# Attention, feed-forward and soft mixture on one core: scores in four quarters of the array, TensorE's order from tile 20 on taken from the program

## The chip, the cores and the metric

The kernel runs on one core of one Trainium2 chip. The core has five engines that work side by side: TensorE (PE, matrix products; its weight loads are listed as PEld), VectorE (DVE), ScalarE (ACT), GpSimd (POOL) and SyncE (SP), which here only issues transfers. Each takes its instructions strictly in the order in which they were put into its queue, and waits at an instruction until what that one needs is there. The metric is the device time of one execution in microseconds (us).

## What is computed

The reference has three stages, each on 3072 tokens of width 512 (4 sequences of 768):

```python
# 1 attention: 32 heads of 64; a query sees 16 keys to either side and 24 block maxima
k_sum = k.reshape(B, H, nb, block, D).max(axis=3)
v_sum = v.reshape(B, H, nb, block, D).mean(axis=3)
scores = concat([where(|i-j| < 16, scale * q @ k.T, -1e9), scale * q @ k_sum.T + log(32)])
x = softmax(scores) @ concat([v, v_sum])
# 2 feed-forward, 512 -> 2048 -> 512
h = x @ w_in;  x = (h * cos(h)) @ w_out
# 3 soft mixture of 8 experts with 4 slots each
logits = x @ phi
d = softmax over tokens(logits);  slot_input = d.T @ x
slot_out[e] = relu(slot_input[e] @ w1[e]) @ w2[e]
out = softmax over slots(logits) @ slot_out
```

All is float32 at the reference's accuracy; the large products are made of three products in the rounded format fp32r (high by high, low by high, high by low).

## The kernel before

**Feed-forward, the trunk.** Six batches b of 512 tokens by 16 slices of the hidden width give 96 tiles s. `mm1(s)` is 12 products of 128x512 into one of two "h" banks of PSUM (L375 to 385); `act1(s)` (L388 to 400) reduces h on DVE (two instructions, L398 and L399) and takes the sine on ACT; `act2(s)` (L403 to 410) multiplies by h on DVE (L405, which frees the h bank), rounds to gh on ACT (L408) and takes the rest gl on POOL (L409); `mm2(s)` (L412 to 423) is 12 products into four acc banks and runs two tiles later. I write H(s) and A(s) for these two dozens of products. `split_w` makes the rounded and the rest part of a slice's weights on ACT (L370) and POOL (L371). In the first 16 tiles the weights are also converted, in three steps on ACT and DVE (L125, L126, L134, L135).

**Background.** Attention is cut into 24 groups g of 8 units (a unit is 64 queries of one sequence against 120 keys, for the two heads of a pair, which lie on rows 0 to 63 and 64 to 127). Groups 0 to 3 are done at the start, the others beside the tiles: scores `att_A(g, j)` in two halves j of four units (8 products 64x64 by 64x120 into one bank, head hh in the array's rows and columns 64*hh; a DVE instruction, L286, scales, adds the mask and writes S), then the row maximum, the exponentials on ACT, the norm, the transposes `att_C` ("tr", L333), the products with v `att_D` ("av", L351). The third stage runs one batch behind: x is transposed ("xt", L447), multiplied by phi ("lt", L455), and so on ("ltt", "dt", "sp"). All of these, and the sums of v ("vs"), share the two banks of one pool, `ps_m`, tag "m": whoever asks for a bank gets the one of the two that was taken longest ago, once its last reader is done.

**What sets the order.** The program emits the tiles in a loop; background work is placed in it by half-steps (two per tile), with a table of offsets (`OC`, `OD`, `MC` and others). The framework's scheduler then orders each engine's queue with a model of its own; in the kernel before it does so for all engines from start to end, so a product of the background can stand anywhere among a tile's products. On the chip this order is fixed.

Of the kernel before, what the change touches and what calls it, by code (L numbers as in the profile page):

```python
# [10 lines left out]
F32 = mybir.dt.float32  # L11
# [4 lines left out]
ALU = mybir.AluOpType  # L16
# [3 lines left out]
B, H, S, D = 4, 8, 768, 64  # L20
# [3 lines left out]
QB = 64  # L24
# [4 lines left out]
KC = KL + NSUM  # L29
# [8 lines left out]
CL = 4  # L38
CP = 0
EE = mybir.EngineType  # L40
MAN = None
PD = 1
PRE = "F I K0 Q0 M K1 Q2 W0 K2 Q1 K3 A B0 Q3 B1 B2 V0 V2 W1 V1 V3 W2 m k0 k1 s0 e0 s2 e2 k2 k3 v X0 X2 X1 X3 s1 t0 e1 s3 t2 e3 d0 t1 d2 t3 d1 d3 c0 G4 G5 W3 c1 W4 c2 w0 c3 W5 a4 a5 f V4 X4 V5 X5 S P"
NACT = 0
NABS = 0
S1 = 1
# [29 lines left out]
def body(ctx: ExitStack, tc: tile.TileContext, q0, qk, kT, vn, vx, w, phi, ex, cst, out):  # L76
    nc = tc.nc
# [5 lines left out]
    m2 = ctx.enter_context(tc.tile_pool(name="m2", bufs=1))  # L83
    ps_acc = ctx.enter_context(tc.tile_pool(name="ps_acc", bufs=1, space=PSUM))
    ps_h = ctx.enter_context(tc.tile_pool(name="ps_h", bufs=2, space=PSUM))
    ps_m = ctx.enter_context(tc.tile_pool(name="ps_m", bufs=2, space=PSUM))
# [3 lines left out]
    att = att_cm.__enter__()  # L90


    NM = 6 * KC
    mask = att.tile([128, 6, KC], F32, name="mask", tag="mask", bufs=1)
    ident = const.tile([128, 128], F32, name="ident")
    sel = const.tile([128, 32 + 256], F32, name="sel")
    avg = const.tile([128, 52], F32, name="avg")
    phis = const.tile([128, 4, 32], F32, name="phis")
# [8 lines left out]
    dsel = sel[:, 0:32]  # L107
# [36 lines left out]
    ksums, vsums, grp = {}, {}, {}  # L144
# [125 lines left out]
            nc.scalar.activation(d["S"][:, u, :], d["ps", j][:, c:c + KC], AF.Exp, bias=d["mx"][:, u:u + 1],  # L270
                                 scale=SCALE, accum_out=d["sm"][:, u:u + 1])

    def att_A(g, j):
        d = grp[g]
        if j == 0:
            if g % 2 == 0:
                grp["S", g // 2] = att.tile([128, 16, KC], F32, name=f"S{g}", tag="S")
            d["S"] = grp["S", g // 2][:, 8 * (g % 2):8 * (g % 2) + 8, :]
        ps = ps_m.tile([128, 512], F32, name=f"sc{g}_{j}", tag="m")
        heads = [slice(64 * hh, 64 * hh + 64) for hh in range(2)]  # L280
        for u in range(4):
            for r in heads:
                t = d["qk"][r, j, u, :]
                nc.tensor.matmul(ps[r, u * KC:(u + 1) * KC], t[:, 0:QB], t[:, QB:], start=True, stop=True)  # L284
        c = (g // 2) % 3
        nc.vector.scalar_tensor_tensor(  # L286
            out=d["S"][:, 4 * j:4 * j + 4, :].rearrange("p w c -> p (w c)"),
            in0=ps[:, 0:4 * KC], scalar=SCALE,
            in1=mask[:, c:c + 4, :].rearrange("p w c -> p (w c)"),
            op0=ALU.mult, op1=ALU.add)  # L290

    def att_max(g, negate=False):
        d = grp[g]
# [48 lines left out]
    def att_D(g):  # L342
        d = grp[g]
        ps = bank(f"av{g}") if g < 4 else ps_m.tile([128, 512], F32, name=f"av{g}", tag="m")
        for j in range(2):
            aT = d["aT", j]
            for u in range(4):
                c = 256 * j + QB * u
                for hh in range(2):
                    r = slice(64 * hh, 64 * hh + 64)  # L350
                    nc.tensor.matmul(ps[r, c:c + QB], d["v"][:, j, u, r],  # L351
                                     aT[:, 128 * u + 64 * hh:128 * u + 64 * hh + 64], start=True, stop=True)
        b, o = g // 4, 256 * ((g // 2) % 2)
        if b not in xh:
            xh[b] = xres.tile([128, 4, TB], F32R, name=f"xh{b}", tag="xh", bufs=2)
            xl[b] = xres.tile([128, 4, TB], F32R, name=f"xl{b}", tag="xl", bufs=2)
        p = 2 * (g % 2)
        ps = ps.rearrange("p (j c) -> p j c", j=2)
        hi, lo = (x[b][:, p:p + 2, o:o + 256] for x in (xh, xl))
        nc.scalar.copy(hi, ps)  # L360
        nc.vector.tensor_tensor(out=lo, in0=ps, in1=hi, op=ALU.subtract)  # L361
# [14 lines left out]
    def mm1(s):  # L376
        f = s % NF
        h = ps_h.tile([128, TB], F32, name=f"h{s}", tag="h")
        hi, lo = wi[f]
        for t in range(4):  # L380
            c = slice(128 * t, 128 * t + 128)
            nc.tensor.matmul(h, hi[:, c], xh[s // NF][:, t, :], start=t == 0, stop=False)  # L382
            nc.tensor.matmul(h, hi[:, c], xl[s // NF][:, t, :], start=False, stop=False)  # L383
            nc.tensor.matmul(h, lo[:, c], xh[s // NF][:, t, :], start=False, stop=t == 3)  # L384
        hps[s] = h

# [25 lines left out]
    def mm2(s):  # L412
        f = s % NF
        gh, gl = gs.pop(s)
        hi, lo = wo[f]
        if f == 0:
            for t in range(4):
                acc[t] = ps_acc.tile([128, 512], F32, name=f"acc{s}_{t}", tag=f"acc{t}")
        for t in range(4):
            c = slice(128 * t, 128 * t + 128)  # L420
            nc.tensor.matmul(acc[t], gh[:, c], hi, start=f == 0, stop=False)  # L421
            nc.tensor.matmul(acc[t], gh[:, c], lo, start=False, stop=False)  # L422
            nc.tensor.matmul(acc[t], gl[:, c], hi, start=False, stop=f == NF - 1)  # L423


# [109 lines left out]
    def at2(h, fn, *a):  # L535
        at(max(h, 0) // 2, max(h, 0) % 2, fn, *a)
# [32 lines left out]
    def masks():  # L569
        nc.vector.tensor_single_scalar(out=ident8, in_=ident, scalar=8.0, op=ALU.mult)  # L570
        nc.scalar.copy(mask_hi, mask)
        nc.gpsimd.tensor_tensor(out=mask_lo, in0=mask, in1=mask_hi, op=ALU.subtract)

    C = lambda t, o, n: (lambda _: nc.sync.dma_start(out=t, in_=cst[:, o:o + n]))
    todo = dict(F=lambda _: fill(F0), f=lambda _: fill(NFILL), I=C(ident, NM, 128), M=C(mask.rearrange("p w c -> p (w c)"), 0, NM),
                A=C(avg, NM + 128, 52), S=C(sel, NM + 180, 288), P=lambda _: nc.sync.dma_start(out=phis.rearrange("p k s -> p (k s)"), in_=phi),
                K=load_kraw, Q=load_q_first, W=load_w, B=lambda i: load_vb(0, i), V=load_v, G=load_qk, X=load_vs,
                m=lambda _: masks(), k=ksum, s=scores, e=exps, v=lambda _: vsum_first(), t=turn, d=att_D, c=convert, c1=conv_1,
                w=lambda f: split_w(f, 0), a=att_K)
    for token in PRE.split():  # L580
        n = token.lstrip("FfIMASPKQWBVGXmksevtdcwa")
        todo[token[:len(token) - len(n)]](int(n or 0))


    for g in range(4, 24):
        h0 = HF[g // 2 % 2] + 2 * NF * (g // 4 - 1) if g > 7 else HB[g // 2 % 2]
        h = h0 + OA * (g % 2)
        if g > 5:
            at2(h - OV, load_v, g)
            at2(h - OV, load_vs, g)  # L590
            at2(h - OK, att_K, g)
        at2(h, att_A, g, 0)
        at2(h + 1, att_A, g, 1)
        if g < 8:
            at2(h + 1, att_max, g, True)
            at2(h0 + OX, att_exps, g)
        else:
            at2(h + 1, att_max, g)
            at2(h + 1, att_sub, g)
            if g % 2:  # L600
                at2(h0 + OX, att_exp, g // 2)
            at2(h0 + OS + 2 * (g % 2), att_sum, g)
        h = h0 + ON + DN * (g % 2)
        at2(h, att_norm, g, nc.gpsimd if g < 8 else None)
        at2(h + OC, att_C, g, 0)
        at2(h + OC + 1, att_C, g, 1)
        at2(h + OD, att_D, g)
        if g + 2 < 24:
            at2(h0 + OQ, load_qk, g + 2)
    for b in range(1, B):  # L610
        s = 8 * (3 * b - 2) - 4
        for i in range(7):
            load, use, k = (load_kraw, ksum, (4 * b + i,)) if i < 4 else (load_vb, vsum, (b, i - 4))
# [31 lines left out]
    for f in range(NPRE, NF):  # L645
        c = max(f - CL, 0)
# [100 lines left out]
    for k in range(4):  # L747
# [3 lines left out]
                                    in1=rz.unsqueeze(1).to_broadcast([128, 4, 32]), op=ALU.mult)  # L751
# [30 lines left out]
    for g in range(2):  # L782
        hp = [ps_acc.tile([128, 512], F32, name=f"hp{g}_{i}", tag=f"acc{2 * g + i}") for i in range(2)]
        for k in range(4):
            for i in range(2):
                for j in range(4):
                    nc.tensor.matmul(hp[i][32 * j:32 * j + 32, :], slT[:, k, :],  # L787
                                     eu[16 * g + 4 * k + j][0][:, 512 * i:512 * i + 512],
                                     start=k == 0, stop=k == 3)
# [9 lines left out]
        for i in range(2):  # L799
            ps = ps_m.tile([128, 512], F32, name=f"ht{g}_{i}", tag="m")  # L800
# [51 lines left out]
def _constants():  # L852

    r = np.arange(128) % QB
    c = np.arange(KL)
    near = np.abs(r[:, None] - (c[None, :] - WIN)) < WIN
    m = np.zeros((128, 6, KC), np.float32)
    for i in range(6):
        ok = near.copy()
        if i == 0:  # L860
            ok[:, c < WIN] = False
        if i == 5:
            ok[:, c >= WIN + QB] = False
        m[:, i, :KL] = np.where(ok, 0.0, -1e9)
        m[:, i, KL:] = np.log(SUMB)
    avg = np.zeros((128, 52), np.float32)
    avg[np.arange(128), 20 + np.arange(128) // SUMB] = 1.0 / SUMB
    s = np.arange(128) % 32
    j = np.arange(128) // 32
    dsel = (s[:, None] == np.arange(32)[None, :]).astype(np.float32)  # L870
    sg = [((s[:, None] == s[None, :]) & ((s // NS) == 4 * g + j)[:, None]).astype(np.float32) for g in range(2)]
    return np.concatenate([m.reshape(128, -1), np.eye(128, dtype=np.float32), avg, dsel, *sg], axis=1)


def _layout(q, k, v, moe_w_in, moe_w_out, moe2_phi, moe2_w1, moe2_w2):
# [45 lines left out]
```

## Time and profile before

| | us |
|---|---|
| median of 3 runs | 801.28 |
| lowest and highest of them | 799.95, 802.89 |
| the profiled execution, its own time | 798.03 |
| its span in the trace | 796.1 |

The first tile's H begins at 48.3 us, H(20) at 212.2 us, and the last product of the trunk ends at 730.3 us; behind it stands the end of the third stage. The profile's page gives busy time for each engine; the views named below give single instructions (start, duration, and in brackets the idle time of the engine just before and what ended it), waits by the instruction that waited, and sums for a stretch. A matmul's duration contains its way through the array; consecutive matmuls overlap, so their cost is the distance of their starts.

### The profile page before, as it was taken

To read this page: it belongs to the slowest core of one execution; us is meant where nothing else is said; L and a number is where in the kernel's file an instruction comes from. 1 tells how busy PE (TensorE), PEld (TensorE's weight loads), DVE (VectorE), ACT (ScalarE), POOL (GpSimd) and SP (SyncE) were. 2 spreads that over 40 slices of the span, in tenths; PEclk is the share of its full clock that TensorE was granted. 3 is DMA by queue.
4 is the path that set the end of the run, shared out by engine and by line. 5 is a ranking of instruction groups with operands and counts; after the bars stand their busy time and mean duration, and the time that the engine had idled before them with its cause. 6 is when DMAs were issued, how large, how long until landed. Compare 5 with 4: busy or idle time off the path is not lost.

```text
span 796.1 us, 13916 instructions
## 1 busy us (share of the span) xinstructions
PE 759.4 (95%) x5517; PEld 588.2 (74%) x5517; DVE 477.1 (60%) x683; ACT 438.2 (55%) x790; POOL 448.0 (56%) x321
## 2 busy tenths in 40 slices
PE   9986878999999999999999999999999999999994
PEld 8865656777787778877778877778787888777453
DVE  5697898447567657467367468574575343443623
ACT  4969867745547546447446456465475445633222
POOL 2575997865655755655547456547557675662000
PEclk9999999999999999999999999999999999999998
DMA  9986565012241021111220020110000842237978
GB/s 314 308 292 225 203 227 197 26 58 71 72 149 39 26 64 39 50 41 62 77 77 26 26 78 25 57 46 26 26 0 27 320 182 80 80 106 283 372 297 265
DMA packets 34672, 98.29 MB, mean 123 GB/s; under 512 B 3376, under 2 KB 13744, under 8 KB 32560
## 3 DMA queue, kind: packets, MB, share of 16 engines
q1 hardware_dynamic: 34608, 97.42, 35.5%
q8 instruction: 43, 0.70, 0.3%
q14 instruction: 21, 0.17, 0.1%
HBM read 89.15 MB, written 6.29 MB: 120 GB/s over the span
## 4 chain that ended last, share of the span: by engine, by line
PE 69%; DVE 12%; DMA 9%; ACT 7%; issue 2%; SPq 0%; ACTq 0%; DVEq 0%
PE h L382 9%; PE acc L421 9%; PE acc L423 9%; PE h L383 9%; PE acc L422 8%; PE h L384 8%; DMA kr<-in_kT_dram 4%; PE sc L284 4%; PE av L351 3%; PE yp L820 2%; DMA raw<-in_w_dram 2%; PE hp L787 2%; PE tr L333 2%; PE xt L447 2%; ACT S L316 2%
## 5 line engine op out<-in xcount | busy, mean ns | idle before, releaser
L371 POOL TENSOR_TENSOR wol<-w,woh 128x512 fp32r<-128x512 f32 x96 | 139.4, 1452 | 106.4 <-ACT woh L370 106.3
L371 POOL TENSOR_TENSOR wil<-w,wih 128x512 fp32r<-128x512 f32 x96 | 130.9, 1364 | 74.6 <-ACT wih L370 73.9
L382 PE MATMUL h<-xh,wih 128*128 128x512 f32 x384 | 155.9, 406 | 10.3 <-DVE a L405 10.3
L409 POOL TENSOR_TENSOR gl<-a,gh 128x512 fp32r<-128x512 f32 x96 | 127.8, 1331 | 64.1 <-ACT gh L408 64.1
L421 PE MATMUL acc<-woh,gh 128*128 128x512 f32 x384 | 150.1, 404 | 4.9 <-ACT gh L408 4.4
L383 PE MATMUL h<-xl,wih 128*128 128x512 f32 x384 | 152.9, 398 | 1.6 <-DVE xl L361 1.6
L384 PE MATMUL h<-xh,wil 128*128 128x512 f32 x384 | 152.4, 397 | 0.0
L422 PE MATMUL acc<-wol,gh 128*128 128x512 f32 x384 | 148.8, 395 | 0.0
L423 PE MATMUL acc<-woh,gl 128*128 128x512 f32 x384 | 146.2, 396 | 0.0
L398 DVE TENSOR_SCALAR a<-h 128x512 f32<-128x512 f32 x96 | 65.8, 685 | 95.4 <-PE h L384 89.8
L400 ACT ACTIVATE a<-a,halfpi 128x512 f32<-128x512 f32 x96 | 69.5, 724 | 86.2 <-DVE a L399 84.3
L370 ACT CAST wih<-w 128x512 fp32r<-128x512 f32 x96 | 59.5, 619 | 84.0 <-PE h L383 83.1
L405 DVE TENSOR_TENSOR a<-h,a 128x512 f32<-128x512 f32 x96 | 66.2, 689 | 65.8 <-ACT a L400 65.8
L382 PEld LDWEIGHTS h<-xh,wih 128*128 128x128 f32 x384 | 72.8, 190 | 30.0 <-DVE a L405 13.3
L421 PEld LDWEIGHTS acc<-woh,gh 128*128 128x128 f32 x384 | 72.5, 189 | 24.1 <-ACT gh L408 5.3
L383 PEld LDWEIGHTS h<-xl,wih 128*128 128x128 f32 x384 | 72.8, 190 | 16.9 <-DVE xl L361 2.2
L384 PEld LDWEIGHTS h<-xh,wil 128*128 128x128 f32 x384 | 72.8, 190 | 16.4 <-POOL w L141 0.3
L422 PEld LDWEIGHTS acc<-wol,gh 128*128 128x128 f32 x384 | 72.8, 189 | 15.7 <-issue 0.5
L423 PEld LDWEIGHTS acc<-woh,gl 128*128 128x128 f32 x384 | 71.6, 188 | 17.1 <-issue 1.4
L408 ACT CAST gh<-a 128x512 fp32r<-128x512 f32 x96 | 59.4, 619 | 31.9 <-DVE a L405 31.5
L370 ACT CAST woh<-w 128x512 fp32r<-128x512 f32 x96 | 59.3, 618 | 23.1 <-PE acc L423 21.4
L399 DVE SCALAR_TENSOR_TENSOR a<-a,h 128x512 f32<-128x512 f32 x96 | 65.7, 684 | 2.4
(138 smaller groups left out, 996.6 us busy)
## 6 DMA issues: line engine op xcount, KB each, us to landing
ex<-in_ex_dram SPq DMA_DIRECT2D x64, 512.0 KB
raw<-in_w_dram SPq DMA_DIRECT2D x16, 1024.0 KB
qk<-in_qk_dram SPq DMA_DIRECT2D x20, 736.0 KB
v<-in_vx_dram SPq DMA_DIRECT2D x24, 384.0 KB
kr<-in_kT_dram SPq DMA_DIRECT2D x16, 384.0 KB
vb<-in_vn_dram SPq DMA_DIRECT2D x12, 512.0 KB
out_dram<-o SPq DMA_DIRECT2D x12, 512.0 KB
v<-vs SPq DMA_DIRECT2D x40, 48.0 KB
```

Source lines behind the costliest of these rows:

```text
L370: nc.scalar.copy(hi, W[f][:, part, :])
L371: nc.gpsimd.tensor_tensor(out=lo, in0=W[f][:, part, :], in1=hi, op=ALU.subtract)
L382: nc.tensor.matmul(h, hi[:, c], xh[s // NF][:, t, :], start=t == 0, stop=False)
L383: nc.tensor.matmul(h, hi[:, c], xl[s // NF][:, t, :], start=False, stop=False)
L384: nc.tensor.matmul(h, lo[:, c], xh[s // NF][:, t, :], start=False, stop=t == 3)
L398: nc.vector.tensor_scalar(out=a, in0=h, scalar1=0.25, scalar2=MAGIC, op0=ALU.add, op1=ALU.add)
L400: nc.scalar.activation(a, a, AF.Sin, bias=halfpi, scale=-TWO_PI)
L405: nc.vector.tensor_tensor(out=a, in0=h, in1=a, op=ALU.mult)
L409: nc.gpsimd.tensor_tensor(out=gl, in0=a, in1=gh, op=ALU.subtract)
L421: nc.tensor.matmul(acc[t], gh[:, c], hi, start=f == 0, stop=False)
L422: nc.tensor.matmul(acc[t], gh[:, c], lo, start=False, stop=False)
L423: nc.tensor.matmul(acc[t], gl[:, c], hi, start=False, stop=f == NF - 1)
```

## The change

From s = 20 on, PE's queue takes its instructions in the order in which the program emits them (`MAN`, `tc.manual_schedule`); the other engines' queues, and PE's up to there, are still the scheduler's. Transposes, av and "dt" are placed two half-steps later (`OC`, `OD`, `MC`). `att_A(g)` is one call for all eight units: both m banks are taken at once, one for each head; the output of unit u lies in rows 64*(u%2) of its head's bank, so that four products in a row take the array's four quarters (row half by head, column half by u%2). S is then ordered by head, with a second mask table (`mask2`, 245 KB, loaded at token N of the start), and `att_D` reads the transposed weights by head from group 4 on. In `mm1` and `mm2` the eight products with the high part of the left factor's weights stand ahead of the four others.

```diff
-MAN = None
+MAN = {EE.PE}
-PRE = "... G4 G5 W3 c1 ..."
+PRE = "... G4 G5 N W3 c1 ..."
-OC = 0
-OD = 3
+OC = 2
+OD = 5
-MC = 1
+MC = 3
...
-    def att_A(g, j):
+    def att_A(g):
...
+        pss = [ps_m.tile([128, 512], F32, name=f"sc{g}_{hh}", tag="m") for hh in range(2)]
+        for n in range(4):
+            for u in (2 * (n % 2), 2 * (n % 2) + 1):
+                for hh in range(2):
+                    t = d["qk"][64 * hh:64 * hh + 64, n // 2, u, :]
+                    o = 64 * (u % 2)
+                    nc.tensor.matmul(pss[hh][o:o + 64, n * KC:(n + 1) * KC], t[:, 0:QB], t[:, QB:], start=True, stop=True)
         c = (g // 2) % 3
...
+        m = mask2[:, c:c + 2, :].rearrange("p w c -> p (w c)").unsqueeze(1).to_broadcast([128, 2, 2 * KC])
+        for hh in range(2):
+            nc.vector.scalar_tensor_tensor(
+                out=d["S"][:, 4 * hh:4 * hh + 4, :].rearrange("p (j w) c -> p j (w c)", j=2),
+                in0=pss[hh][:, 0:4 * KC].rearrange("p (j c) -> p j c", j=2), scalar=SCALE, in1=m,
+                op0=ALU.mult, op1=ALU.add)
...
-                                     aT[:, 128 * u + 64 * hh:128 * u + 64 * hh + 64], start=True, stop=True)
+                    a = d["aT", j][:, 128 * u + 64 * hh:] if g < 4 else d["aT", hh][:, 256 * j + 64 * u:]
+                    nc.tensor.matmul(ps[r, c:c + QB], d["v"][:, j, u, r], a[:, 0:QB], start=True, stop=True)
...
             nc.tensor.matmul(h, hi[:, c], xl[s // NF][:, t, :], start=False, stop=False)
+        for t in range(4):
+            c = slice(128 * t, 128 * t + 128)
             nc.tensor.matmul(h, lo[:, c], xh[s // NF][:, t, :], start=False, stop=t == 3)
...
-        at2(h, att_A, g, 0)
-        at2(h + 1, att_A, g, 1)
+        at2(h, att_A, g)
```

What this does to the queues, at three places. (Line numbers move by 2 to 6: L284 of before is L286 of after, L447 is L453, L382 to L384 are L384, L385 and L388.)

PE, tile 38, before: the first half of the scores of group 14 ("sc14_0", 16 instructions, since each float32 product is issued as two) and the transposes "xt" stand among the products of one tile.

```order
L382 MATMUL h38_3347<-xh2_2059,wih6_3276 128x512
L383 MATMUL h38_3347<-xl2_2060,wih6_3276 128x512
L284 MATMUL sc14_0_3291<-qk14_2890 64x120 x8
L447 MATMUL xt_3301<-ident_86,x2_1896 128x128 x4
L384 MATMUL h38_3347<-xh2_2059,wil6_3277 128x512
L382 MATMUL h38_3347<-xh2_2059,wih6_3276 128x512
```

The second half, "sc14_1", stands 20 rows on, in tile 39. PE, the same place after, the end of the block of scores that stands behind the last product of H(37):

```order
L286 MATMUL sc14_0_3276<-qk14_2894 64x120
L286 MATMUL sc14_1_3277<-qk14_2894 64x120
L453 MATMUL xt_3296<-ident_86,x2_1898 128x128 x4
L425 MATMUL acc32_0_3080<-woh3_3193,gh35_3135 128x512
L426 MATMUL acc32_0_3080<-wol3_3194,gh35_3135 128x512
L425 MATMUL acc32_1_3081<-woh3_3193,gh35_3135 128x512
```

All 16 products of the group (rows like the first two, eight times, heads in turn) now stand in one block, and "xt" directly behind it, ahead of A(35).

DVE, the same group, before (L398, L399 and L405 belong to the tile's h):

```order
L398 TENSOR_SCALAR a37_3284<-h37_3263 128x512
L399 SCALAR_TENSOR_TENSOR a37_3284<-a37_3284,h37_3263 128x512
L405 TENSOR_TENSOR a37_3284<-h37_3263,a37_3284 128x512
L286 SCALAR_TENSOR_TENSOR S14_3290<-sc14_0_3291,mask_85 128x480
L448 COPY x2T_1898<-xt_3301 128x512
L398 TENSOR_SCALAR a38_3368<-h38_3347 128x512
L399 SCALAR_TENSOR_TENSOR a38_3368<-a38_3368,h38_3347 128x512
```

DVE after:

```order
L402 TENSOR_SCALAR a37_3269<-h37_3248 128x512
L403 SCALAR_TENSOR_TENSOR a37_3269<-a37_3269,h37_3248 128x512
L290 SCALAR_TENSOR_TENSOR S14_3275<-sc14_0_3276,mask2_572 128x480
L290 SCALAR_TENSOR_TENSOR S14_3275<-sc14_1_3277,mask2_572 128x480
L409 TENSOR_TENSOR a37_3269<-h37_3248,a37_3269 128x512
```

The two readers of the scores now stand together, behind the two instructions on the h of the tile just finished.

ACT at the start, around the first sine (L400 before, L404 after; "w6" and "cv6" are a weight conversion, S4 exponentials of group 4), before:

```order
L370 CAST wih3_849<-w3_594 128x512
L400 ACT_TABLE_LOAD
L400 ACTIVATE a0_694<-a0_694,halfpi_90 128x512
L125 ACTIVATE w6_883<-raw6_742 128x1024
L126 ACTIVATE cv6_884<-raw6_742 128x1024
L316 ACT_TABLE_LOAD
L316 ACTIVATE S4_698,sm4_800<-S4_698,mx4_719 128x120 x7
L408 CAST gh0_745<-a0_694 128x512
```

ACT after, the same stretch:

```order
L372 CAST wih3_851<-w3_596 128x512
L125 ACTIVATE w6_878<-raw6_754 128x1024
L126 ACTIVATE cv6_879<-raw6_754 128x1024
L319 ACTIVATE S4_700,sm4_802<-S4_700,mx4_721 128x120 x6
L404 ACT_TABLE_LOAD
L404 ACTIVATE a0_696<-a0_696,halfpi_90 128x512
L319 ACT_TABLE_LOAD
L319 ACTIVATE S4_700,sm4_802<-S4_700,mx4_721 128x120 x2
```

Conversion and exponentials have moved ahead of the first sine; gh0, which stood five rows behind that sine, now stands behind the second sine and the next conversion as well:

```order
L404 ACTIVATE a1_798<-a1_798,halfpi_90 128x512
L125 ACTIVATE w7_952<-raw7_829 128x1024
L126 ACTIVATE cv7_953<-raw7_829 128x1024
L319 ACT_TABLE_LOAD
L319 ACTIVATE S4_700,sm5_811<-S4_700,mx5_761 128x120 x6
L412 CAST gh0_757<-a0_696 128x512
```

PE ahead of tile 20, where the order is still the scheduler's, at group 8, before ("sc8_0" is the half of four units, its two heads in turn):

```order
L421 MATMUL acc0_3_900<-woh10_1514,gh10_1479 128x512
L284 MATMUL sc8_0_1672<-qk8_1372 64x120 x8
L382 MATMUL h13_1633<-xh0_464,wih13_1581 128x512
L422 MATMUL acc0_0_897<-wol10_1515,gh10_1479 128x512
L423 MATMUL acc0_0_897<-woh10_1514,gl10_1480 128x512
```

PE after, the same group ("sc8_0" is now one head's eight units):

```order
L388 MATMUL h13_1616<-xh0_464,wil13_1570 128x512 x4
L286 MATMUL sc8_0_1648<-qk8_1374 64x120 x8
L425 MATMUL acc0_0_892<-woh11_1573,gh11_1536 128x512
L286 MATMUL sc8_1_1649<-qk8_1374 64x120 x8
L426 MATMUL acc0_0_892<-wol11_1574,gh11_1536 128x512
```

The eight products of one head stand together, then, one trunk product later, those of the other; the heads no longer stand in turn.

## Rows read from the trace of the kernel before

**Rows 1.** The page: busy time, share and number of instructions of each engine.

```profile
PE 759.4 (95%) x5517; PEld 588.2 (74%) x5517; DVE 477.1 (60%) x683; ACT 438.2 (55%) x790; POOL 448.0 (56%) x321
```

**Rows 2.** Sums by stretch: length, busy time of PE, PEld, DVE, ACT, POOL, clock, DMA.

```profile
48.30:139.70 91.40, 73.29 (x471) 53.90 (x469) 80.17 (x84) 68.13 (x131) 72.58 (x39) 0.94 0.65 229
139.70:212.20 72.50, 71.02 (x470) 55.45 (x468) 41.10 (x58) 41.93 (x79) 48.56 (x36) 1.00 0.18 57
212.20:730.30 518.10, 515.23 (x3282) 407.55 (x3284) 297.51 (x441) 274.43 (x448) 304.04 (x228) 1.00 0.22 74
```

**Rows 3.** Waits of PE from 212.2 to 730.3: us in total, times, longest.

```profile
PE h L382 <- DVE a L405: 2.2, 3, 0.9
PE tr L333 <- DVE S L326: 0.7, 2, 0.5
```

**Rows 4.** Single instructions: start, duration, engine; the trunk's products, nothing between.

```profile
303.46 0.40 PE L382 MATMUL h<-xh,wih 128*128 128x512 f32 x1
306.22 0.40 PE L421 MATMUL acc<-woh,gh 128*128 128x512 f32 x1
```

**Rows 5.** Single instructions: one half of a group's scores, alone among trunk products.

```profile
159.11 0.86 PE L421 MATMUL acc<-woh,gh 128*128 128x512 f32 x3
159.90 1.04 PE L284 MATMUL sc<-qk 64*64 64x120 f32 x16
...
159.90 0.81 PEld L284 LDWEIGHTS sc<-qk 64*64 64x64 f32 x16 [0.36 <-ACT woh L370]
...
160.87 0.50 PE L382 MATMUL h<-xh,wih 128*128 128x512 f32 x1
161.21 0.39 PE L422 MATMUL acc<-wol,gh 128*128 128x512 f32 x1
```

**Rows 6.** Single instructions: two narrow blocks, four and two column groups wide.

```profile
187.44 0.64 PE L184 MATMUL vs<-vb,avg 128*32 128x128 f32 x16
106.36 1.15 PE L351 MATMUL av<-aT,v 120*64 120x64 f32 x32 [1.00 <-DVE vs L195]
```

**Rows 7.** Single instructions of PE and DVE where scores follow a tile's last H product.

```profile
399.19 0.40 PE L384 MATMUL h<-xh,wil 128*128 128x512 f32 x1
399.52 1.04 PE L284 MATMUL sc<-qk 64*64 64x120 f32 x16
399.70 0.69 DVE L398 TENSOR_SCALAR a<-h 128x512 f32<-128x512 f32 x1 [4.19 <-PE h L384]
...
400.49 0.50 PE L421 MATMUL acc<-woh,gh 128*128 128x512 f32 x1
401.03 0.65 DVE L286 SCALAR_TENSOR_TENSOR S<-sc,mask 128x480 f32<-128x480 f32 x1
```

**Rows 8.** Single instructions of ACT at the start, the first sine to the first gh.

```profile
60.22 1.28 ACT L400 ACT_TABLE_LOAD   x1 [0.84 <-DVE a L399]
61.52 0.72 ACT L400 ACTIVATE a<-a,halfpi 128x512 f32<-128x512 f32 x1
62.14 1.11 ACT L125 ACTIVATE w<-raw 128x1024 f32<-128x1024 f32 x1
...
65.59 0.40 ACT L316 ACTIVATE S<-S,mx 128x120 f32<-128x120 f32 x1
68.26 0.60 ACT L408 CAST gh<-a 128x512 fp32r<-128x512 f32 x1
```

**Rows 9.** Waits of PE from 82.5 to 139.7: us in total, times, longest.

```profile
PE h L382 <- DVE a L405: 5.1, 3, 2.8
PE vs L184 <- ACT aT L339: 1.3, 1, 1.3
PE av L351 <- DVE vs L195: 1.0, 1, 1.0
PE tr L333 <- DVE xl L361: 0.9, 1, 0.9
PE sc L284 <- DVE S L286: 0.8, 1, 0.8
```

More of the change, by code (lines that the diff above doesn't have):

```diff
@@ L40 @@
 EE = mybir.EngineType
-MAN = None
+MAN = {EE.PE}
 PD = 1
-PRE = "F I K0 Q0 M K1 Q2 W0 K2 Q1 K3 A B0 Q3 B1 B2 V0 V2 W1 V1 V3 W2 m k0 k1 s0 e0 s2 e2 k2 k3 v X0 X2 X1 X3 s1 t0 e1 s3 t2 e3 d0 t1 d2 t3 d1 d3 c0 G4 G5 W3 c1 W4 c2 w0 c3 W5 a4 a5 f V4 X4 V5 X5 S P"
+PRE = "F I K0 Q0 M K1 Q2 W0 K2 Q1 K3 A B0 Q3 B1 B2 V0 V2 W1 V1 V3 W2 m k0 k1 s0 e0 s2 e2 k2 k3 v X0 X2 X1 X3 s1 t0 e1 s3 t2 e3 d0 t1 d2 t3 d1 d3 c0 G4 G5 N W3 c1 W4 c2 w0 c3 W5 a4 a5 f V4 X4 V5 X5 S P"
 NACT = 0
@@ L271, in first_exps @@
                                  scale=SCALE, accum_out=d["sm"][:, u:u + 1])
-    def att_A(g, j):
+    def att_A(g):
         d = grp[g]
[L275 to L284, printed above, removed]
-        c = (g // 2) % 3
[L286 to L290, printed above, removed]
+        if g % 2 == 0:
+            grp["S", g // 2] = att.tile([128, 16, KC], F32, name=f"S{g}", tag="S")
+        d["S"] = grp["S", g // 2][:, 8 * (g % 2):8 * (g % 2) + 8, :]
+        pss = [ps_m.tile([128, 512], F32, name=f"sc{g}_{hh}", tag="m") for hh in range(2)]
[5 more added lines that the diff above has]
+                    nc.tensor.matmul(pss[hh][o:o + 64, n * KC:(n + 1) * KC], t[:, 0:QB], t[:, QB:], start=True, stop=True)
+        c = (g // 2) % 3
+        m = mask2[:, c:c + 2, :].rearrange("p w c -> p (w c)").unsqueeze(1).to_broadcast([128, 2, 2 * KC])
[4 more added lines that the diff above has]
+                op0=ALU.mult, op1=ALU.add)
     def att_max(g, negate=False):
@@ L345, in att_D @@
         for j in range(2):
-            aT = d["aT", j]
             for u in range(4):
@@ L350, in att_D @@
                     r = slice(64 * hh, 64 * hh + 64)
-                    nc.tensor.matmul(ps[r, c:c + QB], d["v"][:, j, u, r],
-                                     aT[:, 128 * u + 64 * hh:128 * u + 64 * hh + 64], start=True, stop=True)
+                    a = d["aT", j][:, 128 * u + 64 * hh:] if g < 4 else d["aT", hh][:, 256 * j + 64 * u:]
+                    nc.tensor.matmul(ps[r, c:c + QB], d["v"][:, j, u, r], a[:, 0:QB], start=True, stop=True)
         b, o = g // 4, 256 * ((g // 2) % 2)
@@ L422, in mm2 @@
             nc.tensor.matmul(acc[t], gh[:, c], lo, start=False, stop=False)
+        for t in range(4):
+            c = slice(128 * t, 128 * t + 128)
             nc.tensor.matmul(acc[t], gl[:, c], hi, start=False, stop=f == NF - 1)
@@ L572, in masks, with load_mask2 @@
         nc.gpsimd.tensor_tensor(out=mask_lo, in0=mask, in1=mask_hi, op=ALU.subtract)
+    def load_mask2(_):
+        nonlocal mask2
+        mask2 = att.tile([128, 6, KC], F32, name="mask2", tag="mask", bufs=1)
+        nc.sync.dma_start(out=mask2[:, 0:4, :].rearrange("p w c -> p (w c)"), in_=cst[:, NM + 468:NM + 468 + 4 * KC])
+    mask2 = None
     C = lambda t, o, n: (lambda _: nc.sync.dma_start(out=t, in_=cst[:, o:o + n]))
     todo = dict(F=lambda _: fill(F0), f=lambda _: fill(NFILL), I=C(ident, NM, 128), M=C(mask.rearrange("p w c -> p (w c)"), 0, NM),
-                A=C(avg, NM + 128, 52), S=C(sel, NM + 180, 288), P=lambda _: nc.sync.dma_start(out=phis.rearrange("p k s -> p (k s)"), in_=phi),
+                A=C(avg, NM + 128, 52), S=C(sel, NM + 180, 288), N=load_mask2, P=lambda _: nc.sync.dma_start(out=phis.rearrange("p k s -> p (k s)"), in_=phi),
                 K=load_kraw, Q=load_q_first, W=load_w, B=lambda i: load_vb(0, i), V=load_v, G=load_qk, X=load_vs,
@@ L580, in body @@
     for token in PRE.split():
-        n = token.lstrip("FfIMASPKQWBVGXmksevtdcwa")
+        n = token.lstrip("FfIMNASPKQWBVGXmksevtdcwa")
         todo[token[:len(token) - len(n)]](int(n or 0))
@@ L871, in _constants @@
     sg = [((s[:, None] == s[None, :]) & ((s // NS) == 4 * g + j)[:, None]).astype(np.float32) for g in range(2)]
-    return np.concatenate([m.reshape(128, -1), np.eye(128, dtype=np.float32), avg, dsel, *sg], axis=1)
+    m2 = np.concatenate([m[:64, [0, 1, 1, 1]], m[64:, [1, 1, 1, 5]]], axis=0)
+    return np.concatenate([m.reshape(128, -1), np.eye(128, dtype=np.float32), avg, dsel, *sg, m2.reshape(128, -1)], axis=1)
 def _layout(q, k, v, moe_w_in, moe_w_out, moe2_phi, moe2_w1, moe2_w2):
```

## The prediction

> **What bounds the kernel now.** I read the page first. PE is busy 95% of the span, the next engine 60% [rows 1]. The sums by stretch say where that holds: from tile 20 to the end of the trunk PE is busy 515 of 518 us at the full clock while DVE, ACT and POOL have 41 to 47% to spare, and its waits there come to 2.9 us [rows 2, 3]. In that stretch only PE time counts: what a product costs between its neighbours, and any new wait. From 48 to 140 us it is another kernel: PE 73 of 91 us, DVE 80, with conversions of the weights beside the first tiles; there the order on ACT and DVE sets the pace [rows 2]. The end behind 730 us is not touched and moves with the trunk.
>
> The trunk itself cannot gain: between the two instants shown lie 12 products, 2.76 us, so 0.230 each, with nothing idle [rows 4]. Putting eight products with the high part ahead of the four others changes neither number nor distance; gl and the low weights are needed later by up to 8 x 0.230 = 1.8 us, which can only spare a wait.
>
> **The change part by part: scores.** One half of a group's scores, alone: the three products ahead of it start at 159.11, so the last at 159.57; the second product behind it starts at 161.21. Of these 1.64 us two products are trunk (0.46), so the half costs 1.18 us [rows 5]. A group has two, 2.36; from tile 20 on there are 14 groups (10 to 23).
>
> In the half, 16 instructions run as 8 pairs: 1.04 us less the last one's 0.26 is 0.78 for 7 distances, 0.111 a pair [rows 5]. A pair takes two diagonal quarters of the array; now the four quarters come in a row. No row shows four of this form together, so bounds: not under the 0.111 of a pair; at most the 0.222 of two pairs one behind the other. Nearest rows: four column groups of "vs" take (0.64 - 0.27)/3 = 0.122 for a group of four, and the "av" loads, 64 columns each like those of the scores, follow each other at (1.15 - 0.22)/31 = 0.030, four in 0.120 [rows 6]. I take 0.12: eight groups of four instead of eight pairs add 7 x 0.009 = 0.07, and a whole group of scores costs 1.18 + 0.07 = 1.25 in place of 2.36. That is 1.11 x 14 = **-15.5 us**.
>
> Against it stands a loss of shared edges. Entering a narrow block costs 0.33 instead of 0.23 and leaving it 0.34 instead of 0.23, some 0.20 in all [rows 5]; two narrow blocks in a row pay it once. By the two orders there are nine such pairs before and four after, 5 x 0.20 = 1.0, and eleven fewer where a narrow block touches transposes, an estimate of 0.05 each, 0.5. **+1.5 us**.
>
> **The new wait.** A group now takes both "m" banks at once. In eight places (behind the scores of groups 10, 14, 18, 22 "xt", behind 11, 15, 19, 23 "lt") the next thing on PE needs a bank back at once, which before it did not: the other bank was free. The bank comes free when DVE has read the first head, and that reader stands behind the two DVE instructions on the h just finished. The trace has this very sequence, without the bank conflict [rows 7]: last H product 399.19, scores 399.52, DVE's two instructions from 399.70, the reader from 401.03 to 401.68. So "xt" could start at about 401.74. PE is through with half a group at 400.49, with a whole one by the sum above at 400.56. The wait is 1.18 us, and eight are **+9.4 us**. Behind the waiting "xt" stand A's twelve products; nothing hides it, since PE is the bound. Bounds: 0.65 if the reader ran at once (5 us in all), 1.87 if one more DVE instruction like those two (0.69) falls in between (15).
>
> **Old waits and the later placement.** Transposes, av and dt two half-steps later give their suppliers most of a tile more. Of the 2.9 us of waits [rows 3] the 0.7 of "tr" go; of the three on h I take about half: **-1.9 us**, bounds 0 and -2.9. DVE's 4.19 us of idle time ahead of a tile's first instruction [rows 7] is the cover of what is moved; I find no other instruction in the new PE order whose supplier is later than it. Here the sum is -15.5 + 1.5 + 9.4 - 1.9 = **-6.5 us**.
>
> **Ahead of tile 20** the order is still the scheduler's. Most groups there stand head by head (sc8 in the order): two column halves in the same rows, taken as a pair like before, so no gain. But ACT and DVE are reshuffled. A conversion (from 62.14 to 65.59 less a table load of 1.28, 2.2 us) and six exponentials (seven and the gap from 65.59 to 68.26, so 0.38 each, 2.3) now stand ahead of the first sine, which began at 61.52 and had waited 0.84: it comes some 2.2 + 2.3 - 0.84 = 3.7 us later, more if the data of that conversion is late. The first gh, at 68.26, stands behind a second sine, a second conversion and six more exponentials, about 7 us later [rows 8], and the third sine behind two more conversions. I follow that to H(4), 82.0 before: it is late by 4 to 12 us. Behind it PE had 9.1 us of waits up to 139.7 [rows 9], which a late PE no longer has; 8 - 9 would be made good. But part of these waits is itself on DVE's work, and DVE is busy 88% of the stretch [rows 2], so it cannot be pushed together much. I carry **+3 us** into tile 20, bounds -1 (all recovered, a little better) and +12 (nothing recovered). The extra mask, 245 KB on the queue ahead of a weight load, lies within these bounds.
>
> **Sum.** 798.0 - 6.5 + 3 = 794.5 for an execution like the profiled one. That one lay 3.25 us under the median, 801.28 - 798.03, which I add back: **797.8, say 798 us**. So a real gain of 15 us on PE is forecast to be mostly given back, over half in one place: "xt" and "lt" behind scores.
>
> **The rivals.**
> *The start recovers or the wait is shorter.* PE's waits behind H(4), 9.1 us [rows 9], are enough to swallow its delay, or the reader gets ahead of the h instructions. No lag gives 795; with waits of 0.65 too, 790.6. For it: these waits are as long as the middle of the delay.
> *The start does not recover (slower).* The mechanism is the conversion work in front of the first sines and of h's multiplications; if DVE stays full up to tile 12, H(4)'s 12 us stay: 798 + 9 = 807. It turns the result to slower from a lag of about 10.5 us at tile 20. For it: DVE's 80 of 91 us; against: 9.1 us of PE waits behind it.
> *The four quarters do not run together (slower).* If two products of one column half in different rows, or a third in the first one's rows, have to wait, a group of four costs 0.222: 8 x 0.102 = 0.82 more per group, 11.4 in all; but scores that end later meet the reader later too, the wait shrinks from 1.18 to about 0.7, 3.8 less. 798 + 7.6 = 805.6. From 0.22 a group on the change is slower; from about 0.17 on the gain of the scores is halved. Against it: "av" and "vs" start new products in the same rows while earlier ones run, every 0.03 us with durations of 0.22 [rows 6]; for it: no row has two row halves under one column half.
> The Trainium skill, "TensorE: Matmul & The Clock Gate", part 3, says that a weight load overlaps products in flight only when its row group differs. The third quarter has the rows of the first, so by that rule the four would come as two pairs, this rival's time; the "av" row speaks against it, since all its loads share their rows.
> *The wait is longer.* At 1.87 us each, 8 x 0.69 = 5.5 more: 803.5.
>
> **How the numbers follow.** Forecast 0.50, start or wait milder 0.25, start not recovered 0.13, quarters in pairs 0.07, wait longer 0.05. A measurement can tell some 0.5% from no change: under 797.3 is faster, over 805.3 slower. The forecast's own spread (about 4 us either way from start and wait) puts 0.21 of its 0.50 under 797.3; with 0.24 of the milder case faster is 0.45. Slower: 0.08 from the start, 0.04 from the quarters, 0.01 each from the wait and the forecast, 0.14. Same 0.41. The range 790 to 807 leaves out half of the start's case, a third of the quarters', and the best of the mild ones, some 0.15 in all.
>
> **What would show it.** Scores of a group in one block of about 1.04 us from first start to the next product's, quarters starting within some 30 ns: right on the first term; about 1.9 us: pairs. Waits of "xt" and "lt" on DVE's reader (L290), eight of about 1.2: right on the second; none, or PE busy 99% without them, would make the forecast too slow by 9. H(20) at about 214 instead of 212.2 (a group's transposes, 0.9, have moved behind it): right on the start. The trunk's length from H(20) near 512 us, 518 before. Wrong above all would be a wait that I don't list, each us of which counts in full.

## The result and the profile after

The change made the kernel slower: median 808.0 us (806.5 to 810.2, 4 runs) against 801.0 (800.0 to 802.9, 4 runs), ratio 1.011 with a 95% interval of 1.0085 to 1.0139. I had forecast 798 and a range of 790 to 807.

The two profiled executions lie 12.2 us apart (810.23 and 798.03), 5 us more than the medians, since the one of before lies 3 us under its median and the one of after 2 us above; what is compared below is these two, stretch by stretch. The page of after and the sums from tile 20 on (columns as in [rows 1, 2]; the stretch begins with H(20), at 215.1):

```profile
PE 749.5 (93%) x5517; PEld 581.8 (72%) x5517; DVE 466.4 (58%) x683; ACT 440.3 (54%) x790; POOL 449.2 (56%) x321
215.10:742.90 527.80, 506.76 (x3289) 400.81 (x3292) 294.94 (x442) 276.79 (x449) 302.11 (x228) 0.99 0.22 73
```

PE works 8.5 us less from tile 20 on (506.8 for 515.2) and the stretch is 9.7 us longer (527.8 for 518.1): what PE saved, and more, it now waits. The start gave 2.9 (H(20) at 215.1 for 212.2), the end behind the trunk nothing. So the forecast failed in the one stretch that I had priced in detail: there -5.6 us was expected (-6.5, and 0.9 for the transposes that came over the border), +9.7 came, 15.3 off.

PE's waits from tile 20 on, after; they stand against the 2.9 us of [rows 3]:

```profile
PE xt L453 <- DVE S L290: 8.1, 4, 4.6
PE lt L461 <- DVE S L290: 4.7, 4, 1.2
PE acc L425 <- DVE x L448: 4.0, 3, 2.0
PE h L384 <- DVE a L409: 2.8, 1, 2.8
PE vs L184 <- DVE d L501: 1.3, 1, 1.3
```

That is 20.9 us. The first two lines are the wait I had forecast, in the eight places named. Single instructions of PE at one of them, group 14 (start, duration):

```profile
339.85 1.07 PE L388 MATMUL h<-xh,wil 128*128 128x512 f32 x4
340.86 1.05 PE L286 MATMUL sc<-qk 64*64 64x120 f32 x32
343.07 0.66 PE L453 MATMUL xt<-ident,x 128*128 128x128 f32 x4 [1.16 <-DVE S L290]
343.48 0.48 PE L425 MATMUL acc<-woh,gh 128*128 128x512 f32 x1
```

Seven of the eight are 1.16 or 1.17 us long; 1.18 was forecast. The eighth, behind group 10, is 4.60. The rows of DVE and PE there:

```profile
226.18 0.95 DVE L170 TENSOR_REDUCE ks<-kr 128x24 f32<-128x768 f32 x1 [3.10 <-DMA kr<-in_kT_dram]
227.05 0.68 DVE L402 TENSOR_SCALAR a<-h 128x512 f32<-128x512 f32 x1
227.77 0.69 DVE L403 SCALAR_TENSOR_TENSOR a<-a,h 128x512 f32<-128x512 f32 x1
230.30 0.95 DVE L170 TENSOR_REDUCE ks<-kr 128x24 f32<-128x768 f32 x1 [1.84 <-DMA kr<-in_kT_dram]
231.17 1.21 DVE L290 SCALAR_TENSOR_TENSOR S<-sc,mask 128x480 f32<-128x480 f32 x2
231.87 1.11 PE L453 MATMUL xt<-ident,x 128*128 128x128 f32 x4 [4.60 <-DVE S L290]
```

The reader of the scores stands behind a maximum over keys whose data is still on its way: DVE itself sits idle 1.84 us in front of it, and PE behind DVE. The trace of before has such a wait of DVE in the same stretch, with no one on PE waiting for it:

```profile
223.04 0.95 DVE L170 TENSOR_REDUCE ks<-kr 128x24 f32<-128x768 f32 x1 [3.26 <-DMA kr<-in_kT_dram]
```

The third line of the waits is new and I had not listed it. At the turn of a batch the first A needs its acc bank, which is free once x has been copied out of it; DVE and PE there, after:

```profile
314.89 4.20 DVE L329 TENSOR_TENSOR S<-S,rs 128x960 f32<-128x960 f32 x2
319.02 0.68 DVE L402 TENSOR_SCALAR a<-h 128x512 f32<-128x512 f32 x1
319.62 0.68 DVE L448 TENSOR_SCALAR x<-acc 128x512 f32<-128x512 f32 x1
...
320.44 0.47 PE L425 MATMUL acc<-woh,gh 128*128 128x512 f32 x1 [1.09 <-DVE x L448]
```

Two groups' norms, 4.2 us in a row, stand ahead of both copies. Before, there were two norms in a row as well, shorter (2.66 us), and one of the copies stood ahead of them:

```profile
309.55 0.63 DVE L442 TENSOR_SCALAR x<-acc 128x512 f32<-128x512 f32 x1
310.11 0.67 DVE L399 SCALAR_TENSOR_TENSOR a<-a,h 128x512 f32<-128x512 f32 x1
310.70 2.66 DVE L326 TENSOR_TENSOR S<-S,rs 128x960 f32<-128x960 f32 x2
313.28 0.68 DVE L442 TENSOR_SCALAR x<-acc 128x512 f32<-128x512 f32 x1
```

It is the scheduler of DVE that put the norms in front. Which part of the change led it to do so is not shown; the later placement by itself did not (in e1 below a copy still stands first, at 313.62, ahead of the norms at 314.77), nor did PE's fixed order (in e2, without it, the norms stand first, at 309.60). The one wait on h (2.79 us, ahead of 490.11) has two norms, 3.23 us from 482.61 on, ahead of DVE's first instruction on that h too.

Finally two of the waits cost twice. Sums by stretch behind the 4.60 and the 2.79 us wait (clock in the last column but two):

```profile
232.00:238.00 6.00, 6.00 (x51) 4.94 (x52) 4.86 (x6) 1.84 (x5) 1.87 (x2) 0.77 0.23 66
490.10:496.00 5.90, 5.89 (x21) 4.74 (x22) 3.05 (x9) 4.74 (x8) 3.11 (x3) 0.71 0.01 3
```

Behind these waits the granted clock is 0.77 and 0.71 on average: products start 0.427 us apart for some three microseconds, 0.23 after that. At (1 - 0.77) x 6.0 + (1 - 0.71) x 5.9 this is 3.1 us.

### The profile page after: what moved, and what is told of

Same layout as the page of the kernel before. It is cut to its first block, busy times and chain, and to the rows that moved or that the text cites. A ratio compares the mean times of both kernels' runs of the same rounds, so it can differ in the third digit from the quotient of the medians.

```text
span 808.5 us, 13896 instructions
## 1 busy us (share of the span) xinstructions
PE 749.5 (93%) x5517; PEld 581.8 (72%) x5517; DVE 466.4 (58%) x683; ACT 440.3 (54%) x790; POOL 449.2 (56%) x321
## 4 chain that ended last, share of the span: by engine, by line
PE 65%; DVE 13%; DMA 9%; ACT 9%; issue 3%; POOL 1%; SPq 0%; DVEq 0%; ACTq 0%; POOLq 0%
PE h L384 9%; PE acc L425 9%; PE h L385 9%; PE h L388 8%; PE acc L426 8%; PE acc L429 8%; DMA kr<-in_kT_dram 3%; DMA qk<-in_qk_dram 3%; PE av L354 2%; DMA raw<-in_w_dram 2%; PE yp L833 2%; PE hp L800 2%; DVE w L135 2%; PE tr L336 2%; DVE w L134 2%
## 5 line engine op out<-in xcount | busy, mean ns | idle before, releaser
L373 POOL TENSOR_TENSOR wol<-w,woh 128x512 fp32r<-128x512 f32 x96 | 134.0, 1396 | 123.7 <-ACT woh L372 123.6
L384 PE MATMUL h<-xh,wih 128*128 128x512 f32 x384 | 161.0, 420 | 17.9 <-DVE a L409 17.8
L425 PE MATMUL acc<-woh,gh 128*128 128x512 f32 x384 | 154.1, 409 | 5.6 <-DVE x L448 4.0
L385 PE MATMUL h<-xl,wih 128*128 128x512 f32 x384 | 155.6, 405 | 2.0 <-DVE xl L363 2.0
L404 ACT ACTIVATE a<-a,halfpi 128x512 f32<-128x512 f32 x96 | 69.5, 724 | 111.8 <-DVE a L403 111.5
L388 PE MATMUL h<-xh,wil 128*128 128x512 f32 x384 | 105.0, 396 | 0.0
L429 PE MATMUL acc<-woh,gl 128*128 128x512 f32 x384 | 103.7, 392 | 0.1
L384 PEld LDWEIGHTS h<-xh,wih 128*128 128x128 f32 x384 | 75.1, 195 | 37.2 <-DVE a L409 20.7
L385 PEld LDWEIGHTS h<-xl,wih 128*128 128x128 f32 x384 | 75.3, 196 | 17.8 <-DVE xl L363 2.6
L388 PEld LDWEIGHTS h<-xh,wil 128*128 128x128 f32 x384 | 73.3, 191 | 16.5
```

The source lines that it names most:

```text
L373: nc.gpsimd.tensor_tensor(out=lo, in0=W[f][:, part, :], in1=hi, op=ALU.subtract)
L404: nc.scalar.activation(a, a, AF.Sin, bias=halfpi, scale=-TWO_PI)
```

## The experiments

Each was run beside the kernel before on the same chip, and its ratio is to that (medians of before 797.3 to 799.7 us on the three chips used); a stretch "from tile 20 on" is read from each profiled execution, from H(20) to the last A, as 518.1 before and 527.8 after.

**The order alone (e1).** The kernel before with the fixed order and the later placement, scores as they were.

```diff
-MAN = None
+MAN = {EE.PE}
-OC = 0
-OD = 3
+OC = 2
+OD = 5
-MC = 1
+MC = 3
```

> The kernel before, with PE's order taken from the program from tile 20 on and transposes, av and dt two half-steps later, as in the change; scores as before (two halves of four units, one bank each, mask as before). Theory (the bank clash behind the scores and DVE's long jobs in front of readers are what costs): no clash of xt and lt with scores, so those 12.8 us of waits are gone, but scores cost 15 us more than in the change and the waits on x (4.0) stay: about 803 to 808. Rival (the fixed order itself, with the other engines' queues made for another one, is what costs): PE's waits from tile 20 on stay at about 20 us and the time is 812 or more.

Measured 807.0 us, ratio 1.0095 (1.0071 to 1.0119). From tile 20 on (sum and PE's waits):

```profile
211.50:737.70 526.20, 518.19 (x3296) 408.88 (x3296) 293.83 (x442) 276.19 (x449) 300.32 (x228) 1.00 0.22 73
PE xt L447 <- DVE xl L361: 4.5, 4, 3.2
PE tr L333 <- DVE S L326: 1.8, 3, 0.6
...
```

So the fixed order and the later placement together cost 8.1 us with the old scores: 5 more of waits and 3 more of PE's own time; what each of the two costs is not separated. Of the waits 4.5 are of "xt" for a bank again, 3.2 of them behind the second half of group 10. The rival's 20 us of waits did not show; the wait on x, which I expected here, did not show either.

**The change without the fixed order (e2).**

```diff
-MAN = {EE.PE}
+MAN = None
```

> The change with the one line on PE's order taken back: PE's order is the scheduler's from start to end, everything else as changed. Theory (fixed order makes the waits): waits of PE from tile 20 on back to some 3 to 5 us; where the scheduler puts a group's scores head by head they cost as before, so only part of the 15 us stays: 795 to 801. Rival (both banks taken at once by the scores is bad under any order): 804 or more.

Measured 803.2 us, ratio 1.0060 (1.0032 to 1.0088), 522.0 from tile 20 on: between the theory's 795 to 801 and the rival's 804. No wait on the readers of the scores is left, so the eight need the fixed order as well as the two banks. Waits are 11.9 us in all, more than the 3 to 5 that I expected, 4.4 of them on x again: that wait comes from DVE's order, not from PE's.

**xt and lt away from the scores (e3).**

```diff
-MT = 8
+MT = 5
-ML = 14
+ML = 12
-        at2(2 * s + ML + 2, m2_lT, j)
+        at2(2 * s + ML + 1, m2_lT, j)
```

> The change with xt three half-steps earlier (MT 8 to 5), lt two (ML 14 to 12) and ltt one behind lt, so that neither stands behind a group's scores. Theory: the eight waits of xt and lt on the readers of the scores (12.8 us) go, and with the 4.6 us one the stretch at half clock behind it (about 1.4): 808 - 14 = 794. Rival (the waits only move to the next thing that needs a bank, since the scores hold both): 803 or more.

Measured 798.0 us, ratio 0.9982 (0.9964 to 1.0000). From tile 20 on:

```profile
218.70:734.70 516.00, 506.46 (x3279) 397.53 (x3280) 307.58 (x441) 273.06 (x445) 315.32 (x228) 1.00 0.22 75
PE acc L425 <- DVE x L448: 3.6, 3, 1.5
PE vs L184 <- DVE d L501: 2.5, 1, 2.5
PE h L384 <- DVE a L409: 1.9, 3, 0.6
...
```

All eight waits are gone, and little took their place: 12.8 us went, the line behind dt grew from 1.3 to 2.5 and the transposes now wait 1.2; in all PE waits 11.5 us less, and the stretch is 11.8 shorter. The time is 4 us over the 794 that I expected. This is the largest single cause, and three lines undo it.

**The norms one half-step later (e4).**

```diff
-        h = h0 + ON + DN * (g % 2)
+        h = h0 + ON + (g > 7) + DN * (g % 2)
```

> The change with the norms of groups 8 to 23, and the transposes and av behind them, one half-step later. Theory (DVE's two norms, 4.2 us, stand in front of the copy of x out of the acc banks, and the next batch's first A waits): the three waits on x, 4.0 us, go: 804. Rival (DVE's order is the scheduler's and the norms stay in front): 808.

Measured 818.8 us, ratio 1.026 (1.021 to 1.031): neither. The norms stayed in front of the copies and came later themselves, so the wait on x grew from 4.0 to 8.1 us, and the scores came to stand directly behind transposes and waited for those banks (2.6 us). Of the 11.1 us that the stretch is longer than in the change (538.9), waits are 3.9, and half-clock stretches behind them some 4.6. DVE, and the first A behind it:

```profile
318.46 4.26 DVE L329 TENSOR_TENSOR S<-S,rs 128x960 f32<-128x960 f32 x2
...
324.07 0.76 PE L425 MATMUL acc<-woh,gh 128*128 128x512 f32 x1 [2.70 <-DVE x L448]
```

The edit did not do what it was to do, so it does not test the cause; the next one does.

**Copies of x on ACT (e6).**

```diff
-    def x2_out(t):
-        if t % 2:
+    def x2_out(t, every=False):
+        if t % 2 or every:
...
-                last = [x2_out(t) for t in range(4)][3]
+                last = [x2_out(t, s < NSLOT) for t in range(4)][3]
```

> The change, with the copies of x out of the acc banks all on ACT instead of half of them on DVE (but for the last batch). Theory (DVE's two norms in a row, 4.2 us, stand ahead of its copies and A of the next batch waits for the bank): the three waits of A on x, 4.0 us, go, 808 - 4 = 804. Rival (ACT's copies come as late, or h's own instructions on DVE are behind the norms anyway): 807 to 809.

Measured 802.8 us, ratio 1.0061 (1.0038 to 1.0084). The line on x is gone from the waits, the others stand much as they were (8.0 on xt, 4.7 on lt, 3.2 on h, 1.4 behind dt). The stretch is 523.7, 4.1 shorter. The copies' place on DVE, behind the norms, was the cause of these 4.0 us.

**Head by head (e5).** The kernel e3, with the sixteen products of a group ordered by head, so that only column halves alternate.

```diff
-        for n in range(4):
-            for u in (2 * (n % 2), 2 * (n % 2) + 1):
-                for hh in range(2):
+        for hh in range(2):
+            for n in range(4):
+                for u in (2 * (n % 2), 2 * (n % 2) + 1):
```

> The kernel with xt apart (e3), and the scores of a group issued head by head: eight units of the first head, then eight of the second, so that only the two column halves of the array alternate, in the same rows. Theory (the four quarters do run together, and two column halves alone run as a pair): a group costs 2.1 to 2.3 us alone in place of e3's 1.18, 14 groups, +13 to +15 from tile 20 on against e3, so about 811. Rival (what gains is that the block is one and its edges are paid once, the order within it is all the same): a group costs 1.2 to 1.4, the time within 2 us of e3.

Measured 798.0 us, ratio 0.9996 (0.9969 to 1.0024), as a whole no different from e3; but its H(20) came 9.4 us earlier (209.3 for 218.7) and the stretch from there was 5.5 longer (521.5 for 516.0). A group here, and one with quarters after the change:

```profile
334.69 1.08 PE L388 MATMUL h<-xh,wil 128*128 128x512 f32 x4
335.70 1.51 PE L286 MATMUL sc<-qk 64*64 64x120 f32 x32
337.14 0.50 PE L425 MATMUL acc<-woh,gh 128*128 128x512 f32 x1
337.48 0.40 PE L426 MATMUL acc<-wol,gh 128*128 128x512 f32 x1
```

```profile
286.55 1.08 PE L388 MATMUL h<-xh,wil 128*128 128x512 f32 x4
287.57 1.05 PE L286 MATMUL sc<-qk 64*64 64x120 f32 x32
288.55 0.50 PE L425 MATMUL acc<-woh,gh 128*128 128x512 f32 x1
288.88 0.39 PE L426 MATMUL acc<-wol,gh 128*128 128x512 f32 x1
```

Less the two trunk products, a group costs 1.64 us by head and 1.18 by quarters (14 x 0.46 = 6.4). Both expectations missed the cost of a group: the order within the block is worth half a microsecond, not one. (That the whole came within 2 us of e3, as the rival had it, is the start's doing.) The edit does not isolate the column halves, since the two heads overlap: by the single starts in the trace, pairs follow each other every 0.103 us at either end of the block, and from 0.47 to 0.77 us two such trains run at once. One head's eight units by themselves stand in the trace of the change at group 8, ahead of tile 20, where a trunk product parts the heads ("sc8_0" and "sc8_1" in the order):

```profile
163.51 1.04 PE L286 MATMUL sc<-qk 64*64 64x120 f32 x16
164.47 0.50 PE L425 MATMUL acc<-woh,gh 128*128 128x512 f32 x1
164.91 1.04 PE L286 MATMUL sc<-qk 64*64 64x120 f32 x16
```

Each head takes 1.04 us, as much as the diagonal pairs of [rows 5]: two column halves in the same rows do run as a pair. Which bank is written differs as well, and no run separates it: quarters write two banks in turn, both kinds of pairs one.

**All three repairs (e7).** xt and lt away, copies of x on ACT, and dt a half-step earlier (`MC` 3 to 2).

> xt apart (e3), copies of x on ACT (e6) and dt one half-step earlier (MC 3 to 2). Theory: of e3's 9.4 us of waits from tile 20 on the 3.6 on x and the 3.2 on dt's copy go: 798 - 7 = 791, waits there under 3 us; it beats the kernel before by about 1%. Rival: new waits of the same size, 797 to 799.

Measured 792.8 us (790.4 to 795.9), ratio 0.9926 (0.9901 to 0.9951): faster than both kernels. From tile 20 on, 509.9 us with 6.8 of waits:

```profile
215.60:725.50 509.90, 503.14 (x3279) 396.68 (x3278) 302.71 (x433) 275.31 (x453) 315.56 (x228) 1.00 0.22 76
PE h L384 <- DVE a L409: 3.9, 4, 1.2
PE vs L184 <- DVE d L501: 1.8, 1, 1.8
...
```

The wait behind dt did not go as expected (1.8 left), and 2 us of new ones on h came up.

**e7 with the scores of before (e10)** (two halves of four units in diagonal pairs). It is built on the kernel before, so the order of the products within H and A is that kernel's, too.

> e7's order and placement (fixed order, xt, lt and dt apart, x on ACT) with the scores of the kernel before: two halves of four units, diagonal pairs, one bank each. Theory (the quarters are worth what two blocks of 1.17 less one of 1.18 make, 14 x 1.16 = 16 us, less shared edges): the stretch from tile 20 on is 13 to 16 us longer than e7's 510, so 523 to 526. Rival (much of the gain goes into waits for banks even when xt and lt are apart): under 518.

Measured 805.4 us, ratio 1.0095 (1.0066 to 1.0123). From tile 20 on:

```profile
214.10:739.20 525.10, 518.21 (x3286) 407.20 (x3288) 295.01 (x433) 275.53 (x453) 299.05 (x228) 1.00 0.22 73
```

15.2 us more than with quarters, with much the same waits (6.9 for 6.8). That is what the quarters, in one block for two, are worth.

**e7 with the scheduler's order (e9)** (`MAN = None`).

> e7 with PE's order left to the scheduler throughout. Theory (the fixed order costs waits only where a bank or a copy is late; with those three repaired it lets the four quarters stand together in each group, which the scheduler does not): blocks of scores cost more than e7's 1.18 where they stand head by head (1.65 in e5), some 3 to 7 us from tile 20 on, so that stretch is 513 to 517 us against e7's 510. Rival (the scheduler's order is better as such): 510 or less.

Measured 807.4 us, ratio 1.0126 (1.0098 to 1.0154), 524.3 from tile 20 on: 14.4 more than under the fixed order, twice to five times what I expected. PE's own time is 11 us longer and its waits are 10.3. The trace shows where most of the 11 us are: of the fourteen groups nine stand in two blocks of 16 instructions, one in a single block at the pace of e5 and only four in quarters; by the costs above that is 9 x 1.18 + 0.46 = 11.1, less what edges are shared. In e2 four groups stand in two blocks, four between, six in quarters. Why the scheduler parts more groups here than in e2 is open.

**e7 with the order fixed from tile 16 (e8).**

```diff
-        if MAN is not None and s == 20:
+        if MAN is not None and s == 16:
```

> e7 with the fixed order from tile 16 instead of 20. In the change PE lost 3 us between tiles 16 and 20, with two H and two A in one another's midst. Theory (that piece of order of the scheduler's is made for other times): H(20) comes some 2 to 3 us earlier than in e7, 788 to 790. Rival (the wait is for the transposes' copies and the norms at the turn of the batch, whatever the order): the same as e7 or up to 3 us slower.

Measured 802.5 us, ratio 1.0044 (1.0023 to 1.0065). The stretch from tile 20 is the same 510.4, but from H(16) to H(20) it takes 37.0 us (188.1 to 225.1) where e7 takes 29.4. There PE waits 4.55 us for the rounded part of the next batch's x and 1.58 for its rest, and the clock is at half behind the first of these waits. My theory fell: at the turn of the first batch the scheduler's mixture is the better one.

## Why the prediction was wrong

**The scores: right.** The quarters were to give -15.5 us, and e10 against e7 makes it -15.2: a group in quarters costs 1.18 (1.25 was forecast) in place of two halves at 1.18. What the shared edges cost, an estimate of +1.5, is not separated from the rest of PE's own time (below). The rival with quarters in pairs did not come: 32 instructions start within 0.79 us. That two column halves go as a pair, so that groups ahead of tile 20 gain nothing, was right, too (group 8, above). The weight loads there, all for one and the same row half, follow each other without a break while products that last 0.26 us are in flight:

```profile
163.50 0.81 PEld L286 LDWEIGHTS sc<-qk 64*64 64x64 f32 x16 [0.36 <-ACT wih L372]
```

The rule of the Trainium skill ("TensorE: Matmul & The Clock Gate", part 3), that a weight load overlaps products in flight only when its row group differs, does not hold in these rows. Two small terms of the sum are off by rounding (0.7 and half of 2.2 are 1.8, not 1.9; 7 x 0.009 is 0.06, not 0.07), 0.2 us in all.

**The new wait: right in place and size, in seven cases of eight.** 9.4 us were forecast; 12.8 came, the difference in one wait of 4.60. My upper bound allowed for one more DVE instruction like those two on h, and not for a maximum over keys that waits for a transfer, though the trace of before shows one waiting 3.26 us.

**The step that failed** is the sentence "I find no other instruction in the new PE order whose supplier is later than it". I had looked at how much time DVE has to spare on average in a tile (the 4.19 us of [rows 7]) and at the supplier itself, not at the whole queue ahead of it in the changed order of DVE. There the runs show the norms ahead of the copies of x, and dt's copy behind the multiplication of h (e6 shows the first to be the cause; the waits on h and dt are read from the rows alone). The prediction had named this as what would show it wrong above all, a wait that it does not list. Of the 15.3 us that the stretch was off, waits are 10.5 (20.9 for the forecast 9.4 and the 1.0 left of the old ones): 4.0 on x, 3.4 more behind group 10, 2.8 on h, 1.3 on dt's copy, less the 1.0 of old waits that went although I had kept it. Half-clock stretches behind two of these waits are 3.1; I had none in the sum. The rest, 1.7, lies in PE's own time. With the old scores the fixed order and the later placement cost 3.0 of it (e1), where the sum had 1.5 for edges and 0.9 for transposes; and the quarters gave 15.1 of it back (518.2 in e10, 503.1 in e7) for 15.5. That makes 1.0; the last 0.7 is not settled.

**The start: right number, wrong road.** H(20) was forecast at 214 and came at 215.1; H(4) was to be 4 to 12 us late and was 9.5 late. But all of that was made good by H(9) (132.5 for 133.4 before), and the 2.9 us arose anew between tiles 16 and 20 (31.0 us for 27.7), where PE waits 1.83 us at 200.16 and half clock behind it costs another 1.7. PE's three longest waits up to there are all on DVE's multiplication of h: 6.36 us ahead of 70.14, 5.00 ahead of 91.50, 2.46 ahead of 132.50. Of the start no more can be said: eight kernels whose order on every engine is the same up to H(16) (the change, e2, e3, e4, e6, e7, e8, e9) reach H(4) at 89.2 to 92.9 and H(16) at 182.1 to 188.9 in one execution each. Three microseconds there are within what one execution differs from the next.

**The outcome.** Milder waits had 0.25 of my chances, longer ones 0.05; waits not listed had none of their own. With the waits at the size found, 797.8 + 10.5 + 3.1 + 1.7 would have been 813 by my own sum, which starts from profiled executions; the medians are 5 us closer to each other than these.

## What to carry to other kernels

When one engine's order is fixed and the others' is not, walk through each place where the fixed engine takes back a buffer, and read the whole queue of the engine that frees it, transfers and long instructions included; an average of spare time says nothing there. Two buffers taken at once by one step leave none for the next, so put nothing that needs one directly behind it: this cost 12.8 us, and moving xt, lt and what follows lt by two or three half-steps gave back 11.8. A saving on the bound engine is worth its size only in the waits' absence: the quarters saved 15.2 us once xt, lt, x and dt were out of the way (e10 against e7), and the whole went from 1% slower to 0.7% faster without touching them.

## What the runs showed of the hardware

Four 64x64 quarters issued in turn take no longer in all than two diagonal ones did: 32 instructions in 1.05 us here, 16 in 1.04 before [rows 5], so 0.025 us from start to start for 0.052. Two column halves in the same rows take as long as the diagonal pair, 16 in 1.04 (163.51, above). In all three each quarter in use starts an instruction about every 0.103 us, and those in different quarters start some 0.007 us apart (single starts in the traces). In e5's block, 32 in 1.51 us, the second of the two trains of pairs starts 0.47 us behind the first, which runs until 0.77. If it is the second head, its products, in other rows, started before some of the first head's that stood ahead of them in the queue; the trace does not name the head, so this is a reading and not shown.

Behind PE's waits of 4.60 and 2.79 us, the granted clock was at half and products started 0.427 us apart for some three microseconds; behind one of 1.83 us at 200.16 they did too, behind one of 2.02 us at 549.29 they kept 0.23. The length of one wait alone does not tell which it will be.
